# RetNet and gated MLP in one launch: chunks 4 and 5 of the retention in blocks of 64 tokens, in two stages

## Chip, cores and metric

The kernel runs on one core of a Trainium2 chip, in one launch. The metric is device time in microseconds (us); the time of a kernel is the median of its runs. Profiles come from the hardware profiler, one execution each. "Chunk" below always means a chunk of 128 tokens of the retention; "group" means a step of the MLP.

## Reference

The inputs q, k and v have 4 batches, 8 heads, 768 tokens and 64 dimensions each. The first half is a retention with a state that decays, the second an MLP with an activation h * erf(softplus(h)) on 3072 rows of 512:

```python
for t in range(S):
    state = gamma[None, :, None, None] * state + np.einsum('bhd,bhe->bhde', k[:, :, t], v[:, :, t])
    y[:, :, t] = scale * np.einsum('bhd,bhde->bhe', q[:, :, t], state)
...
x = np.ascontiguousarray(attn_out.transpose(0, 2, 1, 3)).reshape(B * S, H * D)
h = x @ w_in
sp = np.maximum(h, 0.0) + np.log1p(np.exp(-np.abs(h)))
g = h * erf(sp)
return (g @ w_out).astype(np.float32)
```

w_in is 512 x 2048 and w_out 2048 x 512. The weights arrive as 64-bit floats and are turned into fp32 on the core.

## The kernel before, in words

**Retention.** A batch has 6 chunks of 128 tokens, so there are 24 chunks, numbered j = 0 to 23; chunks 0 to 5 are batch 0. Keys and queries are scaled by decays up to the chunk's own position (ret_scale, line 404), so that a chunk's additions to the state need no further decay. The heads are handled in four pairs u; the two heads of a pair lie on the two halves of the partitions (r or s is 0 or 1). For chunks 0 to 5 the work is:

- T (ret_transpose, line 425): eight transposes on TensorE, keys into one PSUM tile, queries into another, and two copies on ScalarE into kT and qT.
- S_ (ret_scores, 448): eight matmuls of keys against queries, 128 by 128 scores for each head, into two PSUM tiles.
- M (ret_mask, 461): two VectorE products of 128x512 with the causal mask, into am.
- O_ (ret_out, 469): queries against the state (line 492), values against masked scores (499), and the chunk's additions to the state, keys against values (508), all into two PSUM tiles; the result goes by two ScalarE copies into xT (513). The additions are left out in chunk 5, the last one of its batch.
- A (ret_add, 624): one VectorE addition of 128x256 from PSUM to the state (629).

Chunks 6 to 23 are done by sub_visit (537) in blocks of 64 tokens: scores only within each block of 64 (sub_scores, 519; sub_mask, 527), with the state updated between the two blocks. There the first block's queries meet the old state (559), the additions of both blocks are made (594), the values are applied (574), once into the result's tiles and once ("crossed") into other tiles, the next chunk's scores are made, and the second block's queries meet the state after the first block's addition. VectorE adds the crossed part to the result (617).

**MLP.** Chunks 0 to 3 (512 tokens) go through it in the plain way, in four groups g = 0 to 3 of four hidden tiles: hidden(g, u) makes one hidden tile of 128 x 512 (matmuls on line 682, copy by ScalarE on 700), gate(g) applies softplus and erf on ScalarE, gated(g) multiplies on VectorE (671), project(g, tt) multiplies by w_out (718). From group 4 on, the tokens come in pieces of 256 and the products follow a scheme of seven block products instead of eight (hidden_part, line 775, and project_part, 847), whose sums x_sums and "sums" VectorE makes.

**Order of work.** The order on each engine is written out by hand. The table "after" (line 947) says what follows each hidden(g, u); a list "waiting" is run inside the next hidden or project call by pace_around (656). Chunks 4 and 5 are spread over groups 1 and 2: S_(4) after hidden(1, 3); M(4) inside project(0, 1); O_(4) and A(4) after hidden(2, 0); T(5) after hidden(2, 1); S_(5) and M(5) after hidden(2, 2); O_(5) behind project(1, 0). After O_(5) the small loads of the block decays are issued (load_block_scales, 363).

**Weights and pace.** VectorE and ScalarE turn the weights into fp32 in 16 pieces (conversion, 189). A piece has five steps on VectorE, on lines 221, 225, 230, 233 and 239, and one on ScalarE (222) between the first and the fourth. A counter "room" says how many steps may be put into the queue: pace(n) adds n to it and puts in a step for each full unit; need(...) puts in steps until a named weight is there. So every call of pace in a retention step moves the place of later conversion steps in VectorE's queue. After the fourth step of a piece, the DMA of a later piece is issued on SyncE's queue (load_pieces_after, 183), where it waits for that step. All loads go through SyncE's queue, those of chunks 6 and later (load, 101) as 33 or so small DMAs each.

**PSUM.** Outside of the start, the retention's tiles come from the pool ps_r, which has two tiles ("r") of one bank each, so the third request waits until the first tile's readers are done. The hidden tiles come from ps_h, two tiles ("hp").

Of the kernel before, what the change touches and what calls it, by code (L numbers as in the profile page):

```python
# [12 lines left out]
F32 = mybir.dt.float32  # L13
# [3 lines left out]
ALU = mybir.AluOpType  # L17
PSUM = bass.MemoryType.PSUM

P = 128  # L20
C = 128
TCH = 512
# [7 lines left out]
PAIRS = (0, 2, 1, 3)  # L30
# [15 lines left out]
def kernel(  # L46
# [13 lines left out]
    nc = tc.nc  # L60
    B, H, S, D = q.shape
    d_model, d_ff = w_in.shape
    HP = H // 2
    NC = S // C
# [3 lines left out]
    JPC = TCH // C  # L68
# [6 lines left out]
    const = ctx.enter_context(tc.tile_pool(name="const", bufs=1))  # L75
    loads = ctx.enter_context(tc.tile_pool(name="loads", bufs=3))
    ret = ctx.enter_context(tc.tile_pool(name="ret", bufs=2))
# [8 lines left out]
    KQ, V, KB = {}, {}, {}  # L86
# [14 lines left out]
    def load(j):  # L101
        b, c = divmod(j, NC)
        if j == JPC - 1:

            x = act.tile([P, N], F32, name="e", bufs=1)
            KQ[j] = x[:, : 2 * d_model].rearrange("p (i h d) -> p i h d", i=2, h=H)
            V[j] = x[:, 2 * d_model : 3 * d_model].rearrange("p (h d) -> p h d", h=H)
        else:
            KQ[j] = loads.tile([P, 2, H, D], F32, name="kq")
            V[j] = loads.tile([P, H, D], F32, name="v")  # L110
        now = slice(c * C, (c + 1) * C)
        if j >= NB:
            KB[j] = loads.tile([P, HP * C], F32, name="kb", bufs=2)
            nc.sync.dma_start(KQ[j][:, 0], k[b, :, now, :].rearrange("h p d -> p h d"))
            load_blocks(KQ[j][:, 1].rearrange("p h d -> p (h d)"), q[b, :, now, :])
            load_blocks(KB[j], k[b, :, now, :])
        for i, src in enumerate((k, q) if j < NB else ()):
            nc.sync.dma_start(KQ[j][:, i], src[b, :, now, :].rearrange("h p d -> p h d"))  # L118
        if not early:
            load_values(j)  # L120
# [165 lines left out]
    def pace(n):  # L286

        nonlocal room
        room += n
        while room >= 1:  # L290
            next(weight_steps, None)
            room -= 1
# [37 lines left out]
    for r in range(2):  # L330
        own = slice(r * D, (r + 1) * D)
        nc.gpsimd.tensor_copy(causal_d[own], causal[own, own])
    state = const.tile([P, HP, D], F32, name="state")


    unscale = 1.0 / math.sqrt(D)

# [25 lines left out]
    def load_block_scales():  # L363
        for s, d in itertools.product(range(2), range(2)):
            part = slice((2 * s + d) * 32, (2 * s + d + 1) * 32)
            for u in range(HP):
                nc.sync.dma_start(
                    kq_b[part, 0, 0, u],
                    decay_k[:, 2 * u + s : 2 * u + s + 1].rearrange("(a p) h -> p (a h)", p=32),
                )  # L370
        nc.sync.dma_start(by_b[:, 1], decay_s)
# [12 lines left out]
    QT, KT, SC, AM, XC, SU = {}, {}, {}, {}, {}, {}  # L384
# [12 lines left out]
    def ret_psum(pool=None):  # L397

        pool = pool or (next(psum_turn) if early else ps_r)
        return pool.tile([P, HP, C], F32, name="hp" if pool is ps_h else "r")  # L400
# [118 lines left out]
    def sub_scores(j):  # L519
        for hp in range(HP):  # L520
            for a, s in itertools.product(range(2), range(2)):
                t, own = slice(a * D, (a + 1) * D), slice(s * D, (s + 1) * D)
                nc.tensor.matmul(  # L523
                    SC[j][s][t, hp, :D], KT[j][own, hp, t], QT[j][own, hp, t], start=True, stop=True,
                )

    def sub_mask(j):
        AM[j] = ret.tile([P, 2, HP, C], F32, name="am")
        for s in range(2):
            nc.vector.tensor_tensor(  # L530
                AM[j][:, s, :, :D],
                SC[j][s][:, :, :D],
                causal_d[:, None, :].to_broadcast([P, HP, D]),
                op=ALU.mult,
            )

    def sub_visit(j, g):

# [66 lines left out]
        if j + 1 < NJ:  # L605
            sub_scores(j + 1)
            sub_mask(j + 1)
# [29 lines left out]
    def gate(g):  # L637


        name = "r" if g < 4 and g % 2 else "e"  # L640
        E[g] = act.tile([P, N], F32, name=name, bufs=1)
        nc.scalar.activation(E[g], HS[g], AF.Softplus)  # L642

        if g:
            gate_erf(g)
# [8 lines left out]
    waiting = []  # L654
# [9 lines left out]
    def run(steps):  # L664
        for f, *args in steps:
            f(*args)
# [20 lines left out]
    def hidden(g, u):  # L687
        ft = g * FG + u
        if u == 0:
            HS[g] = act.tile([P, N], F32, name="h")  # L690
        need("in", ft)
        if ft == 0:
            hidden_of(1, slice(TCH - C))
        hidden_of(ft, slice(TCH) if ft > 1 else slice(TCH - C, TCH))

        if ft < FG:
            need("in", ft + 2)
        if ft == 0:
            ret_add(JPC - 1)
        nc.scalar.copy(HS[g][:, u * TCH : (u + 1) * TCH], HP_.pop(ft))  # L700
        done.add(("hidden", ft))
        if ft == FG - 1:
            need("in", FG + 2)
        if g:
            pace_around(3.4 if ft > FG else 0)

    def project(g, tt):
        if g == 0 and tt == 0:
            O[0] = [ps_o.tile([P, d_model], F32, name=f"o{i}") for i in range(TT)]
        step = tt  # L710
        if g:
            of = [(tt, u) for u in range(FG)]
        else:
            of = [(step % 2 * 2 + i // 2, step // 2 * 2 + i % 2) for i in range(4)]
        need("out", g * FG + max(u for _, u in of))
        for tt, u in of:
            ft = g * FG + u
            nc.tensor.matmul(  # L718
                O[0][tt].rearrange("p (d c) -> p d c", d=2),
                E[g][:, u * TCH + tt * P : u * TCH + (tt + 1) * P],  # L720
                w_out_of(ft),
                start=(ft == 0),
                stop=(ft == n_ft - 1),
            )
        if step == TT - 1:
            done.add(("project", g))
        pace_around(3.4)
# [16 lines left out]
    def chunk_of(g):  # L744
        return TCH // SCH + (g - G0) // 2
# [116 lines left out]
    def put_part(m, step):  # L862
# [27 lines left out]
    K_, T, S_, M, O_, A = (  # L890
        ret_scale, ret_transpose, ret_scores, ret_mask, ret_out, ret_add
    )
# [36 lines left out]
    def last_queries():  # L929
# [20 lines left out]
            ([(K_, 4), (need, "in", FG + 3), (load, 5)], []),  # L950
            ([(gate_erf, 0)], []),
            ([(T, 4)], []),
            ([(S_, 4)], []),
        ],
        [
            ([(O_, 4), (A, 4)], []),
            ([(T, 5)], []),
            ([(S_, 5), (M, 5)], []),
            ([], []),
        ],  # L960
        [
# [7 lines left out]
    for g in range(G0):  # L969
        for u in range(FG):  # L970

            if g and u == (2 if g == 1 else 0):
                waiting.append((gated, g - 1))
            hidden(g, u)
            run(after[g][u][0])
            if (g, u) == (1, 0):
                room = 0.0
            waiting.extend(after[g][u][1])
        gate(g)
        if g:  # L980
            for tt in range(TT):
                project(g - 1, tt)
                if g == 1 and tt < 2:
                    waiting.append((K_, 5) if tt else (M, 4))
                elif g == 2 and tt == 0:
                    O_(5)
                    load_block_scales()
                    waiting.append((A, 5))
                elif g == G0 - 1 and tt == 0:
                    waiting.extend([(K_, JPC + 2), (T, JPC + 2)])  # L990
                elif g == G0 - 1 and tt == 1:
                    load(JPC + 4)
# [3 lines left out]
    j = JPC + 2  # L996
    put = None
    for g in range(G0, NG):
        first = g == G0
# [9 lines left out]
        if first:  # L1009
            SC[j] = [ret_psum() for _ in range(2)]  # L1010
            sub_scores(j)
            sub_mask(j)
# [50 lines left out]
    g, m = NG - 1, chunk_of(NG - 1)  # L1063
# [4 lines left out]
    r, t0 = R[m], m * SCH  # L1068
# [50 lines left out]
```

## Time and profile before

| what | us |
|---|---|
| median of five runs | 681.52 |
| lowest and highest run | 681.2, 681.53 |
| the profiled execution's own time | 681.52 |
| its span, first to last instruction | 679.8 |
| TensorE (PE) busy | 673.9 |
| VectorE (DVE) busy | 391.4 |
| ScalarE (ACT) busy | 257.5 |

The profiled execution's time is its span and 1.72 us around it. The granted TensorE clock is 1.00 throughout. How to read a row of the timeline: start in us from the span's beginning, duration in us, engine, line of the kernel, operation, what is written <- what is read by the program's names, the form (partitions x elements), and how many instructions were merged into the row. Square brackets tell how long the engine was idle ahead of the row, and what released it. Merged rows overlap: a row's duration counts to the end of its last instruction, and the next row's first instruction may start before that. Each fp32 matmul stands as two records, a transpose as one. In the row of a matmul the form in front is that of the weights that stand in the array, the one behind it that of the data that is streamed. "PEld" is the loading of the weights, SPq SyncE's queue of DMA issues.

The chip's engines in 40 equal slices of the span (17 us each), in tenths of busy time, as the page has them:

```profile
PE   8999999999999999999999999999999999999998
DVE  5899999576845535634643563555554544343324
```

Chunks 4 and 5 are worked on between 54 and 93 us, in the fourth to sixth slices.

### The profile page before, as it was taken

How to read it: one execution, taken by the hardware profiler on the slowest of the kernel's cores; microseconds unless marked ns; L12 is line 12 of the kernel's file. 1: busy time of each engine (PE TensorE's matmuls, PEld its weight loads, DVE VectorE, ACT ScalarE, POOL GpSimd, SP SyncE). 2: the span in 40 equal slices, each digit the busy share in tenths (PEclk: the TensorE clock that was granted, in tenths of full speed). 3: DMA queues.
4: the chain of work that ended last, by engine and by line, in shares of the span. 5: the costliest groups of instructions: out<-in, count | busy, mean ns of one | idle time of the engine just before them, and what ended most of it. 6: DMA issues, size and time to landing. Idle time of an engine off the chain costs nothing.

```text
span 679.8 us, 14564 instructions
## 1 busy us (share of the span) xinstructions
PE 673.9 (99%) x6264; PEld 575.4 (85%) x6264; DVE 391.4 (58%) x628; ACT 257.5 (38%) x294; POOL 5.5 (1%) x20
## 2 busy tenths in 40 slices
PE   8999999999999999999999999999999999999998
PEld 7744544677999999999999999999999999999996
DVE  5899999576845535634643563555554544343324
ACT  3467363334414324234144143342441441433431
POOL 1000000100000000000000000000000000000000
PEclk9999999999999999999999999999999999999999
DMA  9999644333422212222321222222322300000000
GB/s 193 226 239 257 173 126 103 63 60 61 117 42 49 65 34 44 75 40 40 75 45 34 64 51 41 66 42 46 71 38 45 68 11 1 1 33 1 1 32 31
DMA packets 156512, 47.65 MB, mean 70 GB/s; under 512 B 143008, under 2 KB 147360, under 8 KB 156448
## 3 DMA queue, kind: packets, MB, share of 16 engines
q1 hardware_dynamic: 156032, 46.72, 31.7%
q8 instruction: 49, 0.80, 0.5%
q14 instruction: 15, 0.12, 0.1%
q10 hardware_dynamic: 416, 0.01, 0.0%
HBM read 40.39 MB, written 6.29 MB: 69 GB/s over the span
## 4 chain that ended last, share of the span: by engine, by line
PE 96%; SPq 2%; DMA 1%; DVE 1%; issue 0%; DVEq 0%
PE hp L775 37%; PE o L847 36%; PE o L718 8%; PE hp L682 8%; PE r L559 2%; PE hp L523 1%; SPq L118 1%; DMA w_out_sb<-in_moe_w_in_dram 1%; PE o L594 1%; PE hp L574 1%; PE r L574 1%; SPq L124 1%; PE r L452 0%; PE r L499 0%; PE r L439 0%; PE r L594 0%
## 5 line engine op out<-in xcount | busy, mean ns | idle before, releaser
L775 PE MATMUL hp<-xs,w_in_sb 128*128 128x128 f32 x1280 | 149.7, 275 | 0.0
L775 PEld LDWEIGHTS hp<-xs,w_in_sb 128*128 128x128 f32 x1280 | 147.8, 192 | 1.5 <-issue 0.5
L847 PE MATMUL o<-w_out_sb,h 128*128 128x256 f32 x640 | 141.7, 379 | 0.0
L847 PEld LDWEIGHTS o<-w_out_sb,h 128*128 128x128 f32 x640 | 121.6, 190 | 16.5
L775 PE MATMUL hp<-xT,w_in_sb 128*128 128x128 f32 x960 | 113.7, 275 | 0.0
L775 PEld LDWEIGHTS hp<-xT,w_in_sb 128*128 128x128 f32 x960 | 111.9, 192 | 1.9 <-issue 1.0
L847 PE MATMUL o<-w_out_sb,e 128*128 128x256 f32 x480 | 112.1, 383 | 0.0
L671 DVE TENSOR_TENSOR e<-h,e 128x1024 f32<-128x1024 f32 x42 | 49.5, 1221 | 100.0 <-ACT e L652 100.0
L847 PEld LDWEIGHTS o<-w_out_sb,e 128*128 128x128 f32 x480 | 88.2, 190 | 11.6
L682 PE MATMUL hp<-xT,w_in_sb 128*128 128x512 f32 (+2 forms) x144 | 57.0, 549 | 0.0
L800 DVE TENSOR_TENSOR h<-h,hp 128x512 f32<-128x512 f32 x20 | 13.7, 687 | 72.3 <-PE hp L775 72.3
L642 ACT ACT_TABLE_LOAD x24 | 30.8, 1283 | 60.8 <-issue 45.4
L682 PEld LDWEIGHTS hp<-xT,w_in_sb 128*128 128x128 f32 x144 | 25.5, 190 | 27.1 <-issue 24.2
L652 ACT ACTIVATE e<-e 128x2048 f32<-128x2048 f32 (+1 forms) x23 | 42.1, 1836 | 0.2
L642 ACT ACTIVATE e<-h 128x2048 f32<-128x2048 f32 x22 | 42.0, 1911 | 0.2
L788 DVE TENSOR_TENSOR h<-h,hp 128x512 f32<-128x512 f32 x20 | 13.8, 688 | 41.0 <-PE hp L775 41.0
L793 ACT COPY h<-hp 128x512 f32<-128x512 f32 x20 | 11.7, 587 | 60.6 <-PE hp L775 60.6
L798 ACT COPY h<-hp 128x512 f32<-128x512 f32 x20 | 11.7, 586 | 60.2 <-PE hp L775 60.2
L791 ACT COPY h<-hp 128x512 f32<-128x512 f32 x20 | 11.7, 586 | 57.1 <-PE hp L775 57.1
L615 ACT COPY xT<-r 128x256 f32<-128x256 f32 x33 | 10.8, 375 | 58.1 <-PE r L559 58.1
L652 ACT ACT_TABLE_LOAD x24 | 30.8, 1283 | 0.4
L786 ACT COPY h<-hp 128x512 f32<-128x512 f32 x20 | 11.8, 588 | 48.6 <-PE hp L775 48.6
(140 smaller groups left out, 668.2 us busy)
## 6 DMA issues: line engine op xcount, KB each, us to landing
w_out_sb<-in_moe_w_out_dram SPq DMA_DIRECT2D x14, 512.0 KB, 5.4
kq<-in_k_dram SPq DMA_DIRECT2D x23, 256.0 KB, 4.0
v<-in_v_dram SPq DMA_DIRECT2D x23, 256.0 KB, 3.1
out_dram<-r SPq DMA_DIRECT2D x23, 256.0 KB, 2.9
kq<-in_q_dram SPq DMA_DIRECT2D x288, 16.0 KB, 1.8
kb<-in_k_dram SPq DMA_DIRECT2D x288, 16.0 KB, 1.7
w_in_sb<-in_moe_w_in_dram SPq DMA_DIRECT2D x8, 512.0 KB, 9.2
w_out_sb<-in_moe_w_in_dram SPq DMA_DIRECT2D x8, 256.0 KB, 8.3
```

The lines of the kernel that those rows point to most:

```text
L559: nc.tensor.matmul(pp[r][col * D : (col + 1) * D, u % 2, t], state[own, u, :], QT[j][own, u, t], start=first(r, col), stop=True, skip_grou ...
L574: nc.tensor.matmul(other[a][own, u % 2, D:] if crossed else pp[a][own, u % 2, t], V[j][t, 2 * u + r, :], AM[j][t, r, u, :D], start=crossed ...
L642: nc.scalar.activation(E[g], HS[g], AF.Softplus)
L652: nc.scalar.activation(E[g][:, half], E[g][:, half], AF.Erf)
L671: nc.vector.tensor_tensor(E[g][:, half], HS[g][:, half], E[g][:, half], op=ALU.mult)
L682: nc.tensor.matmul(HP_[ft][:, t], w_in_of(ft, kk), XC[0][:, kk, t], start=(kk == 0), stop=(kk == n_k - 1),)
L718: nc.tensor.matmul(O[0][tt].rearrange("p (d c) -> p d c", d=2), E[g][:, u * TCH + tt * P : u * TCH + (tt + 1) * P], w_out_of(ft), start=(f ...
L775: nc.tensor.matmul(bank[:, u, :], w_in_sb[:, s, IN[a], kk, u * P : (u + 1) * P], XS[m][b][:, kk, :], start=(p in (1, 2, 5) and u == 0 and ...
L786: nc.scalar.copy(h["11"], flat)
L788: nc.vector.tensor_tensor(h["11"], h["11"], flat, op=ALU.add)
L800: nc.vector.tensor_tensor(h["12"], h["12"], flat, op=ALU.add)
L847: nc.tensor.matmul(O[m][i][:, half, :], G[g][a][:, u * P : (u + 1) * P], w_out_sb[:, s, OUT[b], u, :], start=i not in started, stop=(s == ...
```

## The change

Chunks 4 and 5 are done in blocks of 64 tokens too, in two stages, by new functions, without sub_visit's overlap with the next chunk. sub_begin makes the scores within blocks and, in the free half of the same two PSUM tiles, each block's additions to the state; sub_states makes the masked scores and adds the blocks' additions, one after the other, to states in tiles of their own (two new tiles of 128x256, and the state itself at either end); sub_results applies the queries of each block to the state ahead of it and the values to the masked scores, the crossed part into the free half of the result's two tiles; sub_sums adds the crossed part on VectorE. Chunk 5 has additions of its first block only.

They stand where the old steps stood: sub_begin for S_, sub_states for M, sub_results for O_, sub_sums for A. Two places differ: sub_sums(5) runs inside project(1, 3), where A(5) did nothing inside project(1, 1). The amounts for pace differ as shown.

```diff
+    mid = [state] + [const.tile([P, HP, D], F32, name=f"state{i}") for i in range(1, 3)] + [state]
...
+    def sub_additions(j):
+        for u in range(HP):
+            for r in range(2):
+                for a in range(2 if j % NC < NC - 1 else 1):
+                    t, h = slice(a * D, (a + 1) * D), 2 * u + r
+                    nc.tensor.matmul(
+                        SC[j][a][r * D : (r + 1) * D, u, D:], KQ[j][t, 0, h, :], V[j][t, h, :],
+                        start=True, stop=True,
+                    )
+        pace(1)
+
+    def sub_states(j):
+        sub_mask(j)
+        first = 2 * (j - JPC)
+        for a in range(2 if j % NC < NC - 1 else 1):
+            nc.vector.tensor_tensor(
+                mid[first + a + 1], mid[first + a], SC[j][a][:, :, D:], op=ALU.add
+            )
+            pace(-0.4)
+        pace(-0.8)
+
+    def sub_results(j):
+        m, i = divmod(j, JPC)
+        if i == 0:
+            XC[m] = ret.tile([P, HP, TCH], F32, name="xT")
+        pp = [ret_psum() for _ in range(2)]
+        for a in range(2):
+            t, before = slice(a * D, (a + 1) * D), mid[2 * (j - JPC) + a]
+            for u in PAIRS:
+                for r in range(2):
+                    col, own = u // 2, slice(r * D, (r + 1) * D)
+                    nc.tensor.matmul(
+                        pp[r][col * D : (col + 1) * D, u % 2, t], before[own, u, :], QT[j][own, u, t],
+                        start=(a == 0 and u % 2 == 0), stop=False, skip_group_check=True,
+                    )
+        for crossed in range(2):
+            for u in PAIRS:
+                for a in range(2):
+                    r = 1 - a if crossed else a
+                    col, t = u // 2, slice(a * D, (a + 1) * D)
+                    own = slice(col * D, (col + 1) * D)
+                    nc.tensor.matmul(
+                        pp[a][own, 2 + u % 2, :D] if crossed else pp[a][own, u % 2, t],
+                        V[j][t, 2 * u + r, :],
+                        AM[j][t, r, u, :D],
+                        start=False, stop=True, skip_group_check=True,
+                    )
+        for r in range(2):
+            nc.scalar.copy(XC[m][:, r::2, i * C : (i + 1) * C], pp[r][:, :2, :])
+        SC[j] = pp
+        pace(1.4)
+
+    def sub_sums(j):
+        m, i = divmod(j, JPC)
+        for r in range(2):
+            a = 1 - r
+            x = XC[m][:, r::2, i * C + a * D : i * C + (a + 1) * D]
+            nc.vector.tensor_tensor(x, x, SC[j][a][:, 2:, :D], op=ALU.add)
+        pace(-0.6)
+
+    def sub_begin(j):
+        SC[j] = [ret_psum() for _ in range(2)]
+        sub_scores(j)
+        sub_additions(j)
...
-            ([(S_, 4)], []),
+            ([(sub_begin, 4)], []),
...
-            ([(O_, 4), (A, 4)], []),
+            ([(sub_results, 4), (sub_sums, 4)], []),
             ([(T, 5)], []),
-            ([(S_, 5), (M, 5)], []),
+            ([(sub_begin, 5), (sub_states, 5)], []),
...
-                    waiting.append((K_, 5) if tt else (M, 4))
+                    waiting.append((K_, 5) if tt else (sub_states, 4))
                 elif g == 2 and tt == 0:
-                    O_(5)
+                    sub_results(5)
                     load_block_scales()
-                    waiting.append((A, 5))
+                elif g == 2 and tt == 2:
+                    waiting.append((sub_sums, 5))
```

## The prediction

> **What bounds the kernel now.** I read the page first, then the chain that ended last, then TensorE's timeline around chunks 4 and 5, then VectorE's and SyncE's timelines in the same stretch. Of the page the chain's sum by engine:
>
> ```profile
> PE 96%; SPq 2%; DMA 1%; DVE 1%; issue 0%; DVEq 0%
> ```
>
> TensorE carries 96% of the chain (the page has it busy 99%), and the view of waits lists none of its matmuls after 40 us. So a microsecond of matmul time taken out is a microsecond of span, if nothing late takes its place. Now TensorE's timeline over chunks 4 and 5:
>
> ```profile
> 54.09 1.16 PE L452 MATMUL r<-qT,kT 64*128 64x128 f32 x16
> 55.18 14.00 PE L718 MATMUL o<-w_out_sb,e 128*128 128x512 f32 x32
> ...
> 72.54 0.67 PE L492 MATMUL r<-qT,state 64*64 64x128 f32 x16
> 73.14 1.09 PE L499 MATMUL r<-am,v 128*64 128x128 f32 x16
> 74.06 0.63 PE L508 MATMUL r<-v,kq 128*64 128x64 f32 x16
> 74.63 3.70 PE L682 MATMUL hp<-xT,w_in_sb 128*128 128x512 f32 x8
> 78.17 1.04 PE L439 MATMUL r<-ident,kq 128*128 128x128 f32 x8
> ```
>
> Each row starts before the one above it ends: only start-to-start counts. [...]Chunk 4's scores take 55.18 - 54.09 = 1.09 us and its output 74.63 - 72.54 = 2.09. Chunk 5's, in the same timeline, take 83.66 - 82.57 = 1.09 and 92.34 - 90.72 = 1.62 (no additions in the last chunk). Together 5.89 us.
>
> **The price of 64-token blocks** is in the trace already, since chunks 6 to 23 use them:
>
> ```profile
> 135.67 0.69 PE L523 MATMUL r<-qT,kT 64*64 64x64 f32 x32
> 136.29 3.84 PE L775 MATMUL hp<-xs,w_in_sb 128*128 128x128 f32 x32
> ...
> 334.85 0.46 PE L559 MATMUL r<-qT,state 64*64 64x64 f32 x16
> 335.60 0.41 PE L574 MATMUL r<-am,v 64*64 64x64 f32 x16
> 335.83 0.41 PE L574 MATMUL hp<-am,v 64*64 64x64 f32 x16
> 336.07 0.65 PE L523 MATMUL hp<-qT,kT 64*64 64x64 f32 x32
> 336.53 0.41 PE L559 MATMUL r<-qT,state 64*64 64x64 f32 x16
> 336.88 3.72 PE L847 MATMUL o<-w_out_sb,e 128*128 128x256 f32 x16
> ```
>
> Scores by themselves cost 136.29 - 135.67 = 0.62; inside a visit 336.53 - 336.07 = 0.46; so 0.16 is the change back to big matmuls. The two value groups cost 336.07 - 335.60 = 0.47. States at the head and the additions behind them cost 335.60 - 334.85 = 0.75; the same timeline has the additions starting at 335.13, so 0.28 and 0.47. States at the tail cost 0.35, of which 16 records at the score rate (0.46 / 32 = 14.4 ns) are 0.23 and 0.12 is the change back. The last chunk of a batch has half the additions; the visit at 281.61 shows them at 282.07 - 281.61 = 0.46, no cheaper, because one half of the rows then stands idle. I take 0.47 for it too.
>
> **TensorE's sum.** Scores with additions: 0.62 + 0.47 = 1.09, for each chunk. Results: states 0.28 + 0.23, values 0.47, change back 0.12 = 1.10, for each chunk. After: 2 x (1.09 + 1.10) = 4.38. Saved: 5.89 - 4.38 = 1.51 us. By place: nothing in either chunk's scores, which take the additions in; 0.99 in chunk 4's output, 0.52 in chunk 5's. The number of changes between small and big matmuls stays, so their effect on the neighbours (about 0.1 us in the row before or behind) does too.
>
> One rule speaks against this. The Trainium skill, TensorEngine Tiling (Array Packing), Instruction Overhead: each matmul carries about 60 cycles of overhead, so one should not tile along a dimension that is already small. The change makes 128-wide streams into twice as many 64-wide ones. Read as an added cost, a 64-wide record would be (64 + 60) / (128 + 60) = 0.66 of a 128-wide one. L452's 16 records take 1.09 - 0.16 = 0.93, 58 ns each with two abreast; by the rule that is 38 ns, and 19 with four abreast. The four stages fill 64 slots each (chunk 5's half additions count double): 256 x 19 ns = 4.9, plus 4 x 0.14 for the changes = 5.4 us. The rule leaves a gain of 0.5 where the rows give 1.51. I go with the rows: they show this very shape at 14.4 ns.
>
> **VectorE and the pace.** Masks: 1.20 for two 128x512 (L464, 63.86 to 65.06) become 0.67 for two 128x256 (L530). The two state additions in one chain: 0.34 + 0.45 (x_sums' dependent pair, 118.36 to 118.81). Sums: 0.44 for two (L617). The old addition L629 was 0.33. Chunk 4: 1.53 becomes 1.90; chunk 5: 1.20 becomes 1.45. That is 0.62 us more on an engine that is busy without a gap from 69 to 112 us. ScalarE's two copies stay. The room for weight conversion falls: chunk 4 gave 1 - 1.2 + 2.5 - 0.4 = 1.9 and now 0.2, chunk 5 gave 2.3 and now 0.6. So 3.4 conversion steps slide behind other work, none is added. I replayed the counter; for the kernel before it gives VectorE's order exactly as the timeline has it. For the change it says:
> - out3 (w_out's rows for hidden tiles 6 and 7) is ready at 85.2 instead of 84.7; project(1, 0) starts at 86.2 and needs it for its second half, at 88.0. Covered.
> - Chunk 5's masks and state are ready near 86.2, used at 89.7. Covered by 3 us.
> - in7's exponent step on ScalarE now falls behind gate(2) (6.3 us there), so VectorE waits about 0.9 us at 93; the weights have over 5 us of slack by then (VectorE stands idle 7.08 us ahead of 134.06). Covered.
>
> **The one cover that is used up.** The transposes of chunk 5 take the two PSUM tiles of sub_results(4), which are free only after sub_sums(4). VectorE there:
>
> ```profile
> 72.93 2.35 DVE L671 TENSOR_TENSOR r<-h,r 128x1024 f32<-128x1024 f32 x2
> 75.20 1.22 DVE L230 SCALAR_TENSOR_TENSOR w_out_sb<-w_out_sb 128x1024 f32<-128x1024 uint32 x1
> 76.33 0.68 DVE L221 TENSOR_SCALAR w_in_sb<-w_out_sb 128x1024 uint32<-128x1024 uint32 x1
> 76.94 0.41 DVE L629 TENSOR_TENSOR state<-state,r 128x256 f32<-128x256 f32 x1
> ```
>
> After: gated(1) starts 0.26 later (1.46 against 1.20 for masks and additions), ends 75.46; L230 to 76.59; sums (now one step earlier) to about 77.12. TensorE's transposes could start at 78.17 - 0.99 = 77.18. So a stall between 0 (they can't start before the hidden block ends, so no gain) and 0.4 (if the four small operations took 0.42 each unpipelined). I take 0.05, the time from a VectorE end to a TensorE start at 147.87 to 147.92. Behind the waiting transpose stand all later matmuls.
>
> **SyncE.** Its queue issues without a pause from 89.7 us past 150, and it is passed by the moved steps:
>
> ```profile
> 155.30 0.69 DVE L417 TENSOR_TENSOR kb<-kb,kq_b 128x512 f32<-128x512 f32 x1 [4.33 <-DMA kb<-in_k_dram]
> ...
> 163.48 0.69 DVE L788 TENSOR_TENSOR h<-h,hp 128x512 f32<-128x512 f32 x1 [3.43 <-PE hp L775]
> ```
>
> Chunk 8's keys land late and VectorE waits 4.33 us for them. This end is fixed by SyncE's clock, not by TensorE's. Behind them VectorE has 3.43 us to spare. out7's load waits for out4's step, which slides from 99.6 to 100.5, 0.4 behind SyncE's own pace (by_b's issue ended at 100.0). So the landing slips 0.4 while TensorE comes 1.46 earlier: 3.43 - 0.4 - 1.46 = 1.6 us are left. Covered.
>
> **The sum.** 1.51 - 0.05 = 1.46 off. The profiled execution took 681.52 (span 679.8, 1.72 around it), equal to the median of the runs; so 681.52 - 1.46 = 680.06, said as 680.1 us. A measurement of this kernel can tell about 0.2% (1.36 us, so 680.16) from no change; the forecast lies barely beyond it.
>
> **Rivals and chances.**
> - Likeliest, 0.60: as summed, 679.8 to 680.4. About nine tenths of it lie below 680.16.
> - A new wait eats part, 0.22: the transposes wait for sub_sums(4) by 0.3 to 0.9 us, because releases cost more than I take. For: cover of 0.06 us. Against: the two sums are small and ScalarE's copies end near 74.5. Gives 680.4 to 681.0.
> - The change doesn't speed TensorE as it says, 0.08: the 60-cycle rule holds for these stages. 681.52 - 0.5 = 681.0. Against: the visits' rows.
> - Slower, 0.07: out7's load holds SyncE, chunk 8 lands late, VectorE's block of the next stage (no gap from 163.48 to 174.94) holds TensorE's values. With a slip s, the end moves by s - 3.43; it costs as soon as s is over 3.43, and 0.2% from s = 4.8. If ScalarE's gate(2) of 6.3 us stood ahead of out4's step unhidden: +2.9, 684.4. Against: my replay has only in7 behind the gate, with 0.9 of wait.
> - More, 0.03: changes between matmul shapes that vanish, 679.5.
>
> Faster by over 0.2%: 0.54 + 0.03 = 0.57. Within: 0.06 + 0.22 + 0.08 = 0.36. Slower: 0.07. The range leaves out the slower case, the far end and part of the third: 679.7 to 681.0.
>
> **What would show it.** The scores with additions 1.09 us start-to-start, the results 1.10. The wait of chunk 5's transposes for VectorE at 77.2: absent or under 0.1. VectorE's wait for chunk 8's keys grows from 4.33 to about 6.2, its idle ahead of the next L788 row falls from 3.43 to about 1.6. TensorE's first row of the stage that starts at 130.22 starts near 128.8. Wrong, if a TensorE wait over 0.3 us appears behind 55 us, or if a 64-wide group takes over 0.6.

## The result

| | before | after |
|---|---|---|
| median, us | 681.53 (43 runs) | 680.09 (23 runs) |
| lowest and highest | 681.17, 683.25 | 679.71, 681.63 |
| span of the profiled execution | 679.8 | 678.5 |

The ratio is 0.9977, 95% interval 0.9972 to 0.9983: 1.44 us off by the medians, where 1.46 was forecast. The interval lies clear of 1, so the change is faster, by hardly more than the 0.2% that the prediction took as what a measurement can tell. That the medians meet the forecast within 0.02 us is partly luck: the interval reaches from 1.2 to 1.9 us.

Of the page of the changed kernel, the chain's sum by engine; then its TensorE timeline over chunks 4 and 5 (start in us, duration, engine, line, what is done):

```profile
PE 96%; SPq 2%; DMA 1%; DVE 0%; issue 0%; DVEq 0%
```

```profile
54.31 0.69 PE L525 MATMUL r<-qT,kT 64*64 64x64 f32 x32
54.83 0.65 PE L545 MATMUL r<-v,kq 64*64 64x64 f32 x32
55.41 14.00 PE L789 MATMUL o<-w_out_sb,e 128*128 128x512 f32 x32
...
72.77 0.69 PE L573 MATMUL r<-qT,state 64*64 64x64 f32 x32
73.28 0.65 PE L584 MATMUL r<-am,v 64*64 64x64 f32 x32
73.86 3.70 PE L753 MATMUL hp<-xT,w_in_sb 128*128 128x512 f32 x8
77.40 1.04 PE L441 MATMUL r<-ident,kq 128*128 128x128 f32 x8
...
81.80 0.69 PE L525 MATMUL r<-qT,kT 64*64 64x64 f32 x32
82.32 0.64 PE L545 MATMUL r<-v,kq 64*64 64x64 f32 x16
82.89 3.70 PE L753 MATMUL hp<-xT,w_in_sb 128*128 128x512 f32 x8
```

Start-to-start, chunk 4's scores with additions take 55.41 - 54.31 = 1.10 us and its results 73.86 - 72.77 = 1.09; chunk 5's scores with additions take 82.89 - 81.80 = 1.09, and its results, in the same timeline, 91.04 - 89.95 = 1.09. Together 4.37 us; the prediction had 4.38, and before it was 5.89. The retention of these two chunks on TensorE is the whole gain: from the start of chunk 4's scores to the end of chunk 5's output it was 92.34 - 54.09 = 38.25 and is 91.04 - 54.31 = 36.73, so 1.52 less. From there to the end of the span nothing changed (587.46 us in both). This execution came to chunk 4 0.22 us later than that of before, which is why the spans differ by 1.3 only.

VectorE ahead of chunk 5's transposes in the changed kernel:

```profile
73.41 2.35 DVE L742 TENSOR_TENSOR r<-h,r 128x1024 f32<-128x1024 f32 x2
75.68 1.22 DVE L230 SCALAR_TENSOR_TENSOR w_out_sb<-w_out_sb 128x1024 f32<-128x1024 uint32 x1
76.82 0.48 DVE L600 TENSOR_TENSOR xT<-xT,r 128x128 f32<-128x128 f32 x2
```

The sums (L600) stand where the replay of the counter had put them, behind one step. The transposes start at 77.40 = 73.86 + 3.54, the length of the hidden block, with no wait in the row: the cover held. And VectorE where SyncE's late loads arrive:

```profile
155.99 0.69 DVE L419 TENSOR_TENSOR kb<-kb,kq_b 128x512 f32<-128x512 f32 x1 [6.32 <-DMA kb<-in_k_dram]
...
162.18 0.69 DVE L859 TENSOR_TENSOR h<-h,hp 128x512 f32<-128x512 f32 x1 [1.44 <-PE hp L846]
```

The wait for chunk 8's keys is 6.32 us (forecast 6.2), and 1.44 us of idle time are left ahead of the L859 row (forecast 1.6). The view of waits lists none of TensorE's matmuls behind 40 us, and no 64-wide group took more than 0.58 us: neither sign of being wrong appeared.

### The profile page after: what moved, and what is told of

Read it like the earlier page. It is cut to its first block, busy times and chain, and to the rows that moved or that the text cites. A ratio compares the mean times of both kernels' runs of the same rounds, so it can differ in the third digit from the quotient of the medians.

```text
span 678.5 us, 14828 instructions
## 1 busy us (share of the span) xinstructions
PE 672.3 (99%) x6392; PEld 574.4 (85%) x6392; DVE 392.0 (58%) x634; ACT 257.1 (38%) x294; POOL 7.4 (1%) x20
## 4 chain that ended last, share of the span: by engine, by line
PE 96%; SPq 2%; DMA 1%; DVE 0%; issue 0%; DVEq 0%
PE hp L846 37%; PE o L918 36%; PE hp L753 8%; PE o L789 8%; PE r L630 2%; SPq L118 1%; PE hp L525 1%; DMA w_out_sb<-in_moe_w_in_dram 1%; PE o L665 1%; PE hp L645 1%; PE r L645 1%; SPq L124 0%; PE r L525 0%; PE r L441 0%; PE r L665 0%; PE r L573 0%
## 5 line engine op out<-in xcount | busy, mean ns | idle before, releaser
L871 DVE TENSOR_TENSOR h<-h,hp 128x512 f32<-128x512 f32 x20 | 13.7, 687 | 72.3 <-PE hp L846 72.3
L864 ACT COPY h<-hp 128x512 f32<-128x512 f32 x20 | 11.7, 587 | 60.6 <-PE hp L846 60.6
L859 DVE TENSOR_TENSOR h<-h,hp 128x512 f32<-128x512 f32 x20 | 13.8, 688 | 36.0 <-PE hp L846 36.0
L869 ACT COPY h<-hp 128x512 f32<-128x512 f32 x20 | 11.7, 586 | 60.2 <-PE hp L846 60.2
L862 ACT COPY h<-hp 128x512 f32<-128x512 f32 x20 | 11.7, 586 | 57.1 <-PE hp L846 57.1
L866 DVE TENSOR_TENSOR h<-h,hp 128x512 f32<-128x512 f32 x20 | 13.7, 687 | 27.7 <-ACT h L864 27.7
```

Source lines behind the costliest of these rows:

```text
L859: nc.vector.tensor_tensor(h["11"], h["11"], flat, op=ALU.add)
L866: nc.vector.tensor_tensor(h["22"], h["22"], other, op=ALU.add)
L871: nc.vector.tensor_tensor(h["12"], h["12"], flat, op=ALU.add)
```

## The experiments

Three questions were open: whether the gain is TensorE's and where it comes from; how much cover the transposes and SyncE's loads have; and whether the same step pays elsewhere. Medians are compared with those of the kernel before, measured on the same chip.

### Each chunk alone

chunk4_blocks leaves chunk 5 as it was, reading chunk 4's last state tile:

```diff
-                        place(h), state[own, u, :], QT[j][own, u, :],
+                        place(h), (mid[2] if j == JPC + 1 else state)[own, u, :], QT[j][own, u, :],
...
-            ([(sub_begin, 5), (sub_states, 5)], []),
+            ([(S_, 5), (M, 5)], []),
...
-                    sub_results(5)
+                    O_(5)
...
```

> Only chunk 4 in blocks of 64, chunk 5 as before (it reads the state from chunk 4's last tile). If the gain is TensorE's time in the outputs (0.99 us in chunk 4, 0.52 in chunk 5): chunk 4's results 1.10 us start-to-start, 681.53 - 0.99 = 680.5. If the gain came from the order of the conversion steps on VectorE (3.4 steps later, half of them by each chunk): about half of it, 680.8. If it came from fewer changes between matmul shapes inside the output (two in each chunk): half, 680.8, with no difference between the chunks.

chunk5_blocks leaves chunk 4 as it was:

```diff
+    mid = [None, None, state, const.tile([P, HP, D], F32, name="state1")]
...
-            ([(sub_begin, 4)], []),
+            ([(S_, 4)], []),
...
-            ([(sub_results, 4), (sub_sums, 4)], []),
+            ([(O_, 4), (A, 4)], []),
...
```

> Only chunk 5 in blocks of 64, chunk 4 as before. TensorE's time: 681.53 - 0.52 = 681.0, chunk 5's results 1.10 us. The two rivals (order of the conversion steps; changes of shape): about half of the whole gain, 680.8.

Measured against 681.69: chunk 4 alone 680.77 (ratio 0.9989, 0.9980 to 0.9997), chunk 5 alone 681.05 (0.9990, 0.9981 to 0.9999). The intervals are too wide to part 0.99 from 0.52 us; the profiles part them. In chunk4_blocks, chunk 4's results take 74.15 - 73.06 = 1.09 us and TensorE's way from chunk 4's scores to the end of chunk 5's output 91.87 - 54.61 = 37.26, that is 0.99 less than before, to the hundredth. In chunk5_blocks it is 91.69 - 53.97 = 37.72, 0.53 less. So the rivals that had half of the gain in each chunk fall.

chunk4_blocks lost a part again later, in this timeline of its VectorE:

```profile
158.59 0.69 DVE L419 TENSOR_TENSOR kb<-kb,kq_b 128x512 f32<-128x512 f32 x1 [8.09 <-DMA kb<-in_k_dram]
...
163.26 0.68 DVE L859 TENSOR_TENSOR h<-h,hp 128x512 f32<-128x512 f32 x1
```

Chunk 8's keys came at 158.6, the idle time ahead of L859 is gone, and from chunk 5's end to the end of the span it took 679.6 - 91.87 = 587.73 us instead of 587.46. The loss is on TensorE in the crossed values of the next visit, here in the changed kernel and then in chunk4_blocks:

```profile
173.64 0.46 PE L645 MATMUL hp<-am,v 64*64 64x64 f32 x13
174.47 0.70 PE L645 MATMUL hp<-am,v 64*64 64x64 f32 x13
```

0.70 - 0.46 = 0.24 us of the 0.27. That is the path of the slower rival, in an execution that nobody had slowed down.

### Where the time on TensorE comes from

The prediction took 14.4 ns for a 64-wide record from the trace and put it down to four 64x64 quarters of the array at work at once. results_two_abreast takes the pairs in the order 0, 1, 2, 3, so that neighbours use only two quarters (the same edit in the states' and in the values' loop):

```diff
-            for u in PAIRS:
+            for u in range(HP):
...
```

> The changed kernel with the pairs taken in the order 0, 1, 2, 3 in sub_results instead of 0, 2, 1, 3, so that matmuls next to each other fill only two of the four 64x64 quarters of the array; the same instructions in number and size. If it is the four quarters at work at once that make a 64-wide record cost 14.4 ns: each chunk's results 1.10 + 0.92 = 2.0 us, in all +1.84, 681.9, the whole gain gone. If a matmul's own overhead sets the pace (the rule of 60 cycles), the order doesn't matter: 680.1.

680.24 against 681.69 (0.9979, 0.9970 to 0.9988): no loss. TensorE there:

```profile
72.18 0.68 PE L573 MATMUL r<-qT,state 64*64 64x64 f32 x30
72.69 0.22 PE L584 MATMUL r<-am,v 64*64 64x64 f32 x1
72.70 0.22 PE L573 MATMUL r<-qT,state 64*64 64x64 f32 x1
72.70 0.22 PE L584 MATMUL r<-am,v 64*64 64x64 f32 x1
72.70 0.22 PE L573 MATMUL r<-qT,state 64*64 64x64 f32 x1
72.75 0.64 PE L584 MATMUL r<-am,v 64*64 64x64 f32 x30
73.32 3.70 PE L753 MATMUL hp<-xT,w_in_sb 128*128 128x512 f32 x8
```

73.32 - 72.18 = 1.14 us: the order of the column halves is worth 0.05 us at most. This was first read as the end of the four quarters: only the two halves of the rows would work side by side, and a record of 64 output columns by 64 streamed ones would take its half of the rows 28.8 ns. That is the "new theory" of expectations below.

The rows show that it is wrong. In this order the last states (L573) lie on the second half of the columns and the first values (L584) on the first half. Two records of each start within 0.01 us, and the next record starts 0.05 us later: the column halves do work side by side. Two other places say the same. In six_more_issues, a run further down, one matmul's two records have the array to themselves; in the kernel before, the values fill all rows, so that only column halves can work side by side (the view ended at 73.20 and at 73.35 us):

```profile
175.54 0.28 PE L650 MATMUL hp<-am,v 64*64 64x64 f32 x2
```

```profile
73.14 0.33 PE L499 MATMUL r<-am,v 128*64 128x128 f32 x2
73.14 0.44 PE L499 MATMUL r<-am,v 128*64 128x128 f32 x4
```

The lone records start at 175.54 and 175.60: a record that streams 64 columns keeps its quarter for 58 ns, and 14.4 is a fourth of that. The values of before start two by two, at 73.14, 73.30 and 73.41. So results_two_abreast missed its forecast for another reason: the order of the program did not keep TensorE from filling four quarters, because it starts matmuls on a free half ahead of earlier ones on a busy half. halves_in_turn, below, measures how far ahead.

Either way tiles of 64x64 gain nothing by themselves here: the old scores (L452, tiles of 64 rows by 128 columns) start two by two as well, 0.11 us apart for twice the streamed columns, and so filled the array too. What was saved is work that need not be done. scores_in_quarters tests this; the runs behind it ask what fills the array.

scores_in_quarters is the kernel before with the scores of chunks 4 and 5 in 64x64 tiles, but all four blocks:

```diff
+            for b, a, s in itertools.product(range(2), range(2), range(2)):
+                own = slice(s * D, (s + 1) * D)
                 nc.tensor.matmul(
+                    pp[s][a * D : (a + 1) * D, hp, b * D : (b + 1) * D],
+                    KT[j][own, hp, a * D : (a + 1) * D],
+                    QT[j][own, hp, b * D : (b + 1) * D],
                     start=True,
                     stop=True,
                 )
```

> The kernel before, with the scores of chunks 4 and 5 made in 64x64 tiles as in the change, but all four blocks of each head, those across the two blocks of 64 tokens and above the diagonal too. New theory: the gain is the quarter work left out (half of the score blocks, and of the values' products on them), and tiles of 64x64 are worth nothing by themselves: 64 records of 14.4 ns are 0.92, the scores 1.09 as before, 681.5. First reading (four quarters at work at once make small tiles cheap): less than 1.09 for each chunk, 0.16 + 0.46 at best, 680.6.

```profile
54.45 1.16 PE L463 MATMUL r<-qT,kT 64*64 64x64 f32 x64
55.54 14.00 PE L729 MATMUL o<-w_out_sb,e 128*128 128x512 f32 x32
```

1.09 us, as before with a quarter of the instructions; 681.98 against 681.50 (1.0006, 0.9997 to 1.0015: no difference that this can tell). So four times as many matmuls of a quarter of the size cost the same. The four quarters give this too (64 records at 14.4 ns are 0.92 us, and 0.16 for the change back); the expectation was wrong to draw less than 1.09 us from them.

chunk5_both_additions makes chunk 5's second additions too, for nobody:

```diff
-                for a in range(2 if j % NC < NC - 1 else 1):
+                for a in range(2):
```

> The changed kernel with chunk 5's additions of its second block made too (nobody reads them), 16 more records. If the first block's alone keep only one half of the rows busy, these fit beside them: chunk 5's scores with additions 1.09 us as they are, 680.1. If every record costs its 14.4 ns: 1.32, 680.3.

```profile
82.00 0.65 PE L545 MATMUL r<-v,kq 64*64 64x64 f32 x32
82.58 3.70 PE L753 MATMUL hp<-xT,w_in_sb 128*128 128x512 f32 x8
```

0.58 us with 32 records; the changed kernel has 82.89 - 82.32 = 0.57 with 16. The 16 more are free: they fill the half of the rows that the others leave idle. The median is 680.49 against 681.50 (0.9986, 0.9977 to 0.9994); this interval and the changed kernel's overlap.

rows_in_turn puts r, and a for the values, in the outer loop, so that four matmuls (eight records) of one half of the rows follow each other:

```diff
-            for u in PAIRS:
-                for r in range(2):
+            for r in range(2):
+                for u in PAIRS:
...
-            for u in PAIRS:
-                for a in range(2):
+            for a in range(2):
+                for u in PAIRS:
```

> The changed kernel with sub_results' matmuls ordered so that all of one half of the rows come first (r, and a for the values, in the outer loop), then all of the other half; the same instructions. New theory: only the two halves of the rows work at once, each taking one 64-column record in 28.8 ns; the two halves of the columns don't add to that. Then a group of 32 records takes 0.92 us instead of 0.46, each chunk's results 1.10 + 0.87 to 0.92, in all +1.7 to 1.85, 681.9. If each record had its own price of 14.4 ns whatever runs beside it: 680.1.

680.30 against 681.50 (0.9984, 0.9975 to 0.9993), and chunk 4's results take 73.86 - 72.72 = 1.14 us: the expected loss did not come. As for the columns, the expectation had left out that TensorE looks ahead. In the rows, states of one half and values of the other start in the same hundredths:

```profile
73.24 0.22 PE L584 MATMUL r<-am,v 64*64 64x64 f32 x1
73.24 0.22 PE L573 MATMUL r<-qT,state 64*64 64x64 f32 x1
```

halves_in_turn puts all 32 records of one half ahead of all 32 of the other:

```diff
+        for half in range(2):
+            for a in range(2):
...
+                        pp[half][col * D : (col + 1) * D, u % 2, t], before[own, u, :], QT[j][own, u, t],
...
+            for crossed in range(2):
...
+                        V[j][t, 2 * u + r, :],
```

> The changed kernel with sub_results ordered so that all its matmuls on the first half of the rows come first (32 records: states of both blocks, values and crossed values), then all on the second half. In the run with the rows in turn, four matmuls at a time, the two halves overlapped all the same. If TensorE starts matmuls of one half while up to 8 records of the other are in front of them, but not 32: each chunk's results near 2.0 us, in all +1.7, 681.8. If it runs ahead that far too, or if the halves are not what is shared: 1.10 each, 680.1. In between: a run-ahead of some records.

```profile
72.73 0.68 PE L573 MATMUL r<-qT,state 64*64 64x64 f32 x16
73.24 0.46 PE L583 MATMUL r<-am,v 64*64 64x64 f32 x10
73.49 0.27 PE L573 MATMUL r<-qT,state 64*64 64x64 f32 x2
...
74.00 0.63 PE L583 MATMUL r<-am,v 64*64 64x64 f32 x16
74.57 3.70 PE L752 MATMUL hp<-xT,w_in_sb 128*128 128x512 f32 x8
```

Now the loss is there: 74.57 - 72.73 = 1.84 us for each chunk, 0.75 more, and 681.58 against 681.52 (1.0001, 0.9992 to 1.0010), the gain gone. The first 16 records, alone on one half of the rows with both column halves, take 73.24 - 72.73 = 0.51 us where 32 on four quarters take 0.51 in the changed kernel. From 73.49, the second half's states (L573) start while the last values of the first half (L583) are still to come, so TensorE does start matmuls ahead of others when they lie on the other half. How far, the rows count: at 73.49 ten of the first half's 16 values had started, so the first of the states passed six records, three matmuls. An estimate agrees: without any overlap of the row halves 64 records, two at a time for 58 ns, would take 1.84, and with the start and the change back (0.05 and 0.12, from the visits' rows) 2.01; measured are 1.84, so 0.17 us, six records or so on each half, ran side by side. In rows_in_turn and results_two_abreast the first matmul of the other half stands behind eight records, two of which start at once; a reach of six is enough there. In all these kernels the two row halves write to different PSUM tiles; whether they would also work side by side on one tile is not shown.

### The cover of the transposes

old_pace has the amounts of pace as they were before:

```diff
-            pace(-0.4)
-        pace(-0.8)
+        pace(-1.2)
...
-        pace(1.4)
+        pace(2.5)
...
-        pace(-0.6)
+        pace(-0.4 if j == JPC else 0)
```

> The changed kernel with the amounts of pace as they were (1.9 for chunk 4, 2.3 for chunk 5 instead of 0.2 and 0.6). In VectorE's queue one more step (L221, 0.60 us) then stands ahead of chunk 4's sums. If chunk 5's transposes wait for these sums with 0.1 us to spare: a TensorE wait of 0.5 us at 77.4, 680.6. If the order of the steps has slack everywhere: 680.1. If the lower pace carries the gain: 681.5.

sums4_late runs chunk 4's sums one call later:

```diff
-            ([(sub_results, 4), (sub_sums, 4)], []),
+            ([(sub_results, 4)], [(sub_sums, 4)]),
```

> The changed kernel with chunk 4's sums one call later, inside hidden(2, 1); in VectorE's queue two conversion steps (L221 and L233, 0.60 + 1.25 us) then stand ahead of them. If chunk 5's transposes wait for the sums to free their PSUM tiles, with 0.1 us to spare: a TensorE wait of 1.75 us at 77.4, and 680.1 + 1.75 = 681.85, slower than before. If the transposes don't depend on them: 680.1.

TensorE of old_pace, TensorE of sums4_late, and the sums on VectorE of the two:

```profile
77.59 1.09 PE L441 MATMUL r<-ident,kq 128*128 128x128 f32 x8 [0.23 <-DVE xT L599]
```

```profile
78.89 1.09 PE L441 MATMUL r<-ident,kq 128*128 128x128 f32 x8 [1.34 <-DVE xT L600]
```

```profile
77.26 0.48 DVE L599 TENSOR_TENSOR xT<-xT,r 128x128 f32<-128x128 f32 x2
78.56 0.48 DVE L600 TENSOR_TENSOR xT<-xT,r 128x128 f32<-128x128 f32 x2
```

Both wait for VectorE's sums, as expected. Against the end of the hidden block (73.65 + 3.54 = 77.19 and 73.85 + 3.54 = 77.39) the transposes start 0.40 and 1.50 us late. Medians: 680.46 against 681.69 (0.9983, 0.9974 to 0.9991) and 681.87 against 681.62 (1.0002, 0.9993 to 1.0010). So the lower pace is not where the gain comes from, and two conversion steps put ahead of two small sums (which moves them from 76.82 to 78.56, by 1.74 us) give back the gain of the whole change. The cover is about 0.25 us, not the 0.06 of the prediction: in both runs the transposes start 0.33 us behind the start of the sums, which in the changed kernel would be at 77.15, and there the hidden block ends at 77.40. In sums4_late the transposes start at 78.89, behind the first sum (78.56 + 0.29) and ahead of the end of the second (79.04). The first tile they need is free after one of the two.

### SyncE's queue

six_more_issues delays SyncE by six small loads that nothing reads:

```diff
+        for i in range(6):
+            nc.sync.dma_start(
+                more[:32, i], decay_k[:, i : i + 1].rearrange("(a p) h -> p (a h)", p=32)
+            )
```

> The changed kernel with six more small loads (into a tile that nothing reads) on SyncE's queue behind by_b's, 0.56 us each, so that the loads of chunks 6 to 8 slip by 3.4 us. If the slower rival's path is real and has 1.44 us to spare (VectorE's idle time ahead of L859 in the profile after): VectorE waits 9.7 us for chunk 8's keys instead of 6.3, none is left before L859, TensorE's crossed values behind it wait, and the end moves by 3.4 - 1.44 = 1.9 us, 682.0. If TensorE has slack of its own there (PSUM tiles, order): less, 680.1 at the least.

Its VectorE and its TensorE:

```profile
160.08 0.69 DVE L424 TENSOR_TENSOR kb<-kb,kq_b 128x512 f32<-128x512 f32 x1 [10.19 <-DMA kb<-in_k_dram]
...
164.75 0.68 DVE L864 TENSOR_TENSOR h<-h,hp 128x512 f32<-128x512 f32 x1
```

```profile
165.49 3.84 PE L851 MATMUL hp<-xs,w_in_sb 128*128 128x128 f32 x32 [1.40 <-DVE h L864]
...
176.28 0.40 PE L650 MATMUL hp<-am,v 64*64 64x64 f32 x11 [0.47 <-DVE h L876]
```

The path is real: the keys land late, VectorE has no idle time left, TensorE waits 1.40 us for a PSUM tile and 0.47 at the crossed values, 1.87 in all, where 1.9 were expected. The median is 683.11 (682.0 expected) against 681.62 (1.0027, 1.0013 to 1.0042), with runs from 681.66 to 686.26. The profiled execution took 682.61; what the longer runs lost more was not profiled.

loads_earlier gives this path more room:

```diff
-            ([(sub_begin, 5), (sub_states, 5)], []),
+            ([(sub_begin, 5), (sub_states, 5), (load_block_scales,)], []),
...
-                    load_block_scales()
+                    load(6)
...
-            ([(load, 6)], []),
+            ([], []),
```

> The changed kernel with SyncE's queue in another order: the loads of the block decays behind sub_states(5) instead of behind sub_results(5), and chunk 6's loads in their old place, ahead of out7's load that waits for out4's step. Chunk 8's keys then land about 7 us earlier. If the late keys cost time in part of the executions (their landing moved by up to 2.6 us between profiles of kernels with the same order, and only 1.44 us were to spare): 0.1 to 0.3 us off the median, 679.8 to 680.0, and fewer runs above 680.3. If 1.44 us to spare is enough: 680.1. If out7's later load holds VectorE's conversion and chunk 6: slower, 680.5.

```profile
154.30 0.69 DVE L419 TENSOR_TENSOR kb<-kb,kq_b 128x512 f32<-128x512 f32 x1 [4.70 <-DMA kb<-in_k_dram]
...
162.10 0.69 DVE L859 TENSOR_TENSOR h<-h,hp 128x512 f32<-128x512 f32 x1 [3.06 <-PE hp L846]
```

The keys land only 1.7 us earlier than in the changed kernel, not 7: chunk 8's own loads keep their place behind chunk 7's, and out7's load now stands between chunks 6 and 7. The idle time doubles to 3.06, and the median is 680.18 against 681.52 (0.9980, 0.9971 to 0.9989), the same as the changed kernel's. So in most executions this path costs that kernel nothing; whether it makes the few long ones (up to 681.63), these 11 runs can't tell.

### The same step for chunk 3

chunk3_too does chunk 3 in blocks as well, with the three state tiles used in turn:

```diff
+    mid = 2 * ([state] + [const.tile([P, HP, D], F32, name=f"state{i}") for i in range(1, 3)])
...
-    S_(3)
+    sub_begin(3)
...
-    M(3)
+    sub_states(3)
...
-    ret_out(JPC - 1, lambda: hidden_of(0, slice(TCH - C)), state_last=True)
+    hidden_of(0, slice(TCH - C))
+    sub_results(JPC - 1)
+    sub_sums(JPC - 1)
```

> The changed kernel with chunk 3 in blocks too, its steps in the places of the old ones, three state tiles used in turn. If TensorE sets the time there as it does for chunks 4 and 5: another 0.99 us, 679.1. If the conversion of the first weights on VectorE sets it (hidden tile 1 needs its second half at 29.45, and the two state additions and the sums stand ahead of or among these steps): nothing gained, 680.1 to 680.6.

680.49 against 681.62 (0.9984, 0.9975 to 0.9992): nothing gained over the changed kernel. Its TensorE behind chunk 3's results:

```profile
28.31 11.90 PE L756 MATMUL hp<-xT,w_in_sb 128*128 128x384 f32 x40 [0.48 <-DVE w_in_sb L239]
```

In the changed kernel this block starts at 28.23. What TensorE saved, it waits for VectorE's first weights. The saving is worth something only where TensorE is the late one.

## Why the prediction was right

**TensorE's sum**: right in each place (forecast 0, 0.99, 0, 0.52; measured -0.01, 1.00, 0, 0.53). It was made from rows that show the same shapes in the same kernel, and the reason given with it, four quarters at work at once, is what the single starts show (58 ns for each record, four at a time). By the runs the account is this. Scores: 0.92 becomes 0.46, since the two blocks across the chunk's halves are left out; values the same, 0.92 to 0.46. States and additions cost 0.46 each before and after. So chunk 4 saves 0.92; chunk 5 saves 0.92 less the 0.46 of the additions that it didn't have. The 0.07 more that each shows belongs, as an estimate, to the change of shape inside the old output: its states took 0.60 to the first value, where 16 records are 0.46 and a start in the visits 0.05.

**The rule of 60 cycles** (the Trainium skill, TensorEngine Tiling (Array Packing), Instruction Overhead), read as an added cost, would have left 0.5 us. In scores_in_quarters, 64 narrow records take the 1.09 us of 16 wide ones; the rule read so doesn't hold for these matmuls, and the rows were the right choice.

**Chunk 5's half additions** were taken at 0.47 from a row, with the reason that one half of the rows stands idle. Measured 0.46 to 0.57 by where one cuts (82.89 - 82.32 has the change back in it), and chunk5_both_additions shows the reason to be true.

**VectorE**: masks and additions 65.55 - 64.10 = 1.45 us (forecast 1.46), busy time of the page 391.4 to 392.0 (0.62 forecast). The order of the steps was that of the replay, and VectorE waited 0.99 us for in7's exponent step (0.9 forecast), at no cost.

**The transposes' cover** was the term that was mis-sized: 0.06 us forecast, about 0.25 measured, so the 0.05 us of stall did not come. The forecast took both sums to end before the first tile is free.

**SyncE's slip**: forecast 0.4, measured 0.69 at chunk 8's keys. The block decays' 16 issues alone took 9.49 us instead of 8.92. SyncE's issue times vary from one execution to the next more than the change moves them: the same 16 loads of chunk 6's keys took 7.5 to 9.3 us in these runs' profiles. The forecast had no term for that; chunk4_blocks paid 0.27 us for it.

## What to carry to other kernels

Price a matmul shape from a row of the same shape in the same trace, start-to-start, and then ask by a run with all the work in the new shape whether the shape or the omitted work is the gain; here it was the omitted work. A run with the matmuls in another order does not disprove that parts of the array work side by side, since TensorE starts some of them ahead of their turn; look at where single records start. When a step's saving is near 1 us, look for the two or three covers that it uses up on other queues and say how much each has left: two VectorE steps, 1.74 us together, put ahead of two small sums gave all of it back. A saving pays only where its engine is the late one: chunk 3's, 26 us earlier, paid nothing.

## What was not expected of the hardware

For fp32 matmuls the quarters of the array work side by side, by rows and by columns: a record of 64 by 64 that streams 64 columns keeps its quarter for 58 ns, and up to four start within 0.02 us. It is not the order of the program alone that fills them. Matmuls on a free half start ahead of earlier ones on a busy half: runs of eight records on either half of the rows overlapped fully (1.14 us for 64 records), runs of 32 only by about six on each.
